# Sliding-window attention feeding a two-matmul network: which engine adds 1e-9 to the softmax sums

## The chip, the cores and the metric

One core of one Trainium2 chip runs the whole program. The metric is the device time of one execution in microseconds (us). A core has five engines that matter here, each with its own queue of instructions worked off in order: TensorE (PE in the rows, PEld for its weight loads), VectorE (DVE), ScalarE (ACT), GpSimd (POOL) and SyncE (SP), which here only issues DMAs. Engines wait for each other through semaphores.

## The reference

Attention over 4 batches, 8 heads, 768 positions, head size 64, with 4 sink keys and a window of 128 keys; then a network with weights 512 by 2048 and 2048 by 512 on the 3072 resulting rows.

```
scores = q @ k.T / sqrt(64);  scores outside sink and window = -1e9
a = exp(scores - max(scores));  a = a / (sum(a) + 1e-9)
x = (a @ v), heads side by side: 3072 x 512
h = x @ w_in;  g = h where h >= 1, 0 where h <= -1, (h+1)^2/4 between
out = g @ w_out
```

All inputs are float32; the weights arrive as 64-bit words and are decoded on the chip.

## The kernel before, in words

The work is cut into 8 chunks of 384 rows (`CT` = 3 tiles of 128 rows). For each chunk the attention of 8 heads is computed, one "unit" for each head, so there are 64 units; then the chunk goes through the network in 16 steps (`NJ`) of 128 hidden columns. Precision is kept by splitting operands in a high part and a rest and multiplying three combinations.

TensorE's queue is written out by hand: `attn_steps` lists the attention pieces of a unit, `moe_steps` those of the network, and `spread` weaves the attention of the next chunk into the network of the present one by fixed costs. The queues of the other engines are ordered by the planner of the framework, which runs its own model of the times when the program is built and puts an instruction where the model has it ready; `queue` and `issue_after` fix that order only in the first part of the program.

Units 0 to 15 take a plain path in pairs (`pair_scores` and the functions after it); there `pair_diag` adds the 1e-9 on VectorE already (L445) and takes the reciprocal behind it (L446). Units 16 to 63 take the "split" path, 48 units:

- `load` fetches q and k by DMA; ScalarE rounds them (L259, L262), VectorE forms the rest of k (L261; GpSimd does so for units 16 to 19), GpSimd the rest of q (L263).
- `scores` runs three times for a unit: two matmuls into a PSUM tile `ps_a` (L277), VectorE's masked maximum (L281, which frees that `ps_a` tile), ScalarE's exponential with the sum as a by-product (L284, an activation and a read of its accumulator). After the third one come the addition of 1e-9 to the three sums of each row (L289, GpSimd), the reciprocal (L290, VectorE), then VectorE's scaling of the probabilities (L296 or L298, the latter an operation with a read of its accumulator) and of the sink part (L301).
- `transp` turns the probabilities around on TensorE (L336, L337) into a `ps_a` tile; ScalarE copies it (L339, L341), VectorE forms the rests (L340, L342), GpSimd cuts two triangles out of each part with selects (L345, L347) and spreads the sinks (L349).
- `values` fetches v; ScalarE rounds it (L313, L318) and GpSimd forms the rests (L314, L319).
- `av` multiplies with v on TensorE (L383); L384 to L386 add the two halves.
- `recheck`, in units 24 to 55, copies one element on GpSimd (L229), re-reads a weight tile by DMA and folds it in on ScalarE and VectorE (L233, L235).

There are three `ps_a` tiles, taken in turn by scores, transposes and values; a matmul into one waits until its last readers are done.

The network of a chunk is `stage1` (L571 on TensorE, L578 and L579 on ScalarE, L580 on VectorE, L581 on ScalarE, L582 on VectorE or GpSimd) and `stage2` (L590 on TensorE). The weights are decoded early by L164 to L177.

Of the kernel before, what the change touches and what calls it, by code (L numbers as in the profile page):

```python
# [13 lines left out]
ALU = mybir.AluOpType  # L14
# [5 lines left out]
CT = 3  # L20
# [29 lines left out]
def attn_ffn(ctx, tc, qk, qkp, vx, vs, par, w_in, w_out, out):  # L50
    nc = tc.nc
# [214 lines left out]
    def scores(u, i):  # L266
        b, h, t0 = u
        qs, k_s = st["qk", u]
        if i == 0:
            st["p", u] = [att.tile([P, CT, 260], F32, name="p"), att.tile([P, 2 * CT], F32, name="stat")]  # L270
        p, stat = st["p", u]
        t = t0 + i
        lo = KB if t == 0 else 0
        c0 = i * KB if t0 else max(0, (i - 1) * KB)
        ps = ps_a.tile([P, 512], F32, name="ps_a")
        for j, q in enumerate(qs):
            nc.tensor.matmul(ps[:, lo:260], lhsT=q[:, i * P:(i + 1) * P], rhs=k_s[:, c0:c0 + 260 - lo],  # L277
                             start=(j == 0), stop=(j == len(qs) - 1))
        peak_i = peak[:, units.index(u), i:i + 1]
        m = (m0, m1, m2)[min(t, 2)]  # L280
        nc.vector.tensor_tensor_reduce(  # L281
            out=p[:, i, lo:260], in0=ps[:, lo:260], in1=m, scale=-0.125, scalar=3.0e38,
            op0=ALU.add, op1=ALU.min, accum_out=peak_i)
        nc.scalar.activation(p[:, i, lo:260], p[:, i, lo:260], AF.Exp, bias=peak_i, scale=-1.0,  # L284
                             accum_out=stat[:, i:i + 1])
        if i < CT - 1:
            return
        st.pop(("qk", u))
        nc.gpsimd.tensor_scalar(stat[:, CT:2 * CT], stat[:, 0:CT], 1.0e-9, None, op0=ALU.add)  # L289
        nc.vector.reciprocal(stat[:, CT:2 * CT], stat[:, CT:2 * CT])  # L290
        i0 = int(t0 == 0)

        for i in range(CT):
            r, own = stat[:, CT + i:CT + i + 1], p[:, i, KB:260]
            if t0 + i == 0:
                nc.vector.tensor_scalar(own, own, r, None, op0=ALU.mult)  # L296
            else:
                nc.vector.tensor_tensor_reduce(out=own, in0=own, in1=p[:, i, 0:P], scale=r, scalar=0.0,  # L298
                                               op0=ALU.add, op1=ALU.add, accum_out=stat[:, i:i + 1])
        sk = att.tile([P, CT * NSINK], F32, name="sk")[:, :(CT - i0) * NSINK]  # L300
        nc.vector.tensor_tensor(sk.rearrange("p (i s) -> p i s", s=NSINK), p[:, i0:, P:KB],  # L301
                                stat[:, CT + i0:2 * CT].unsqueeze(2).broadcast_to([P, CT - i0, NSINK]), op=ALU.mult)
        st["p", u] = (p, sk)
# [244 lines left out]
    def attn_steps(n):  # L548
        us = {k: units[n - k] for k in (-1, 0, 1, 2) if 0 <= n - k < len(units)}
        steps = []  # L550
        if n == NATIVE:
            steps.append((0.0, lambda: load(us[0])))
        if -1 in us:
            steps.append((0.0, lambda: load(us[-1])))
        if 1 in us and n - 1 >= NATIVE:
            steps.append((0.0, lambda: values(us[1])))
        steps += [(0.22, lambda i=i: scores(us[0], i)) for i in range(CT) if 0 in us]
        steps += [(0.43, lambda: transp(us[1]))] if 1 in us and n - 1 >= NATIVE else []
        steps += [(1.0, lambda: av(us[2]))] if 2 in us and n - 2 >= NATIVE else []
        if n in CHECK:  # L560
            steps.append((0.0, lambda: recheck(n - CHECK[0], n)))
        return steps
# [243 lines left out]
```

## Time and profile before

| what | us |
|---|---|
| median of three runs | 717.24 (717.17 to 718.19) |
| the profiled execution, its time | 716.97 |
| the profiled execution, span from first to last instruction | 715.2 |
| TensorE busy | 686.7 |
| VectorE busy | 517.2 |
| ScalarE busy | 496.2 |
| GpSimd busy | 291.5 |

All durations below come from the profiled execution. Its time is 1.8 us more than its span and 0.27 us less than the median of the runs. A row "start, us, engine line operation" gives the start from the beginning of the span and how long it took; a bracket tells how long the engine sat idle before it and what ended the wait. The mean granted TensorE clock is 0.995 of full speed.

### The profile page before, as it was taken

The numbers are of one execution on the slowest core, as the hardware profiler recorded it, in microseconds if no ns is written. First come the engines' busy times: TensorE is split into PE (matmuls) and PEld (weight loads), VectorE is DVE, ScalarE is ACT, GpSimd is POOL, SyncE is SP. The second block draws the span as 40 slices with busy tenths as digits, with TensorE's granted clock in tenths as the row PEclk, the third lists the DMA queues.
The fourth block names the chain that finished last, engine by engine and source line by source line (L and its number), as shares of the span: only waits on it lengthen the run. The fifth ranks groups of instructions, "written<-read, shape, count | busy, mean of one in ns | idle before, by whom it ended". The sixth has DMA issues, their size and how long they took to land.

```text
span 715.2 us, 12306 instructions
## 1 busy us (share of the span) xinstructions
PE 686.7 (96%) x3873; PEld 606.6 (85%) x3873; DVE 517.2 (72%) x1414; ACT 496.2 (69%) x1289; POOL 291.5 (41%) x509
## 2 busy tenths in 40 slices
PE   6689998999999999999999999999999999999996
PEld 3367776799999999999899988999999999989995
DVE  8988997887776878688777787778777777732221
ACT  5786777687677878787677777778776866544332
POOL 2002334754452555366455465646554454400000
PEclk9999999999999999999999999999999999999998
DMA  8854524132243344244433443324422220001001
GB/s 270 278 170 158 177 91 142 52 102 57 58 147 103 117 123 126 65 161 128 110 92 96 141 127 116 111 97 156 120 60 65 80 69 16 8 1 45 1 0 49
DMA packets 44841, 73.04 MB, mean 102 GB/s; under 512 B 13024, under 2 KB 29408, under 8 KB 44768
## 3 DMA queue, kind: packets, MB, share of 16 engines
q1 hardware_dynamic: 41504, 59.59, 27.3%
q10 hardware_dynamic: 3264, 12.58, 5.0%
q8 instruction: 33, 0.54, 0.3%
q14 instruction: 40, 0.33, 0.1%
HBM read 65.87 MB, written 6.29 MB: 101 GB/s over the span
## 4 chain that ended last, share of the span: by engine, by line
PE 76%; DVE 8%; ACT 6%; POOL 3%; DMA 3%; issue 2%; ACTq 0%; SPq 0%; POOLq 0%; DVEq 0%
PE o_ps L590 32%; PE h_ps L571 31%; PE ps_a L383 5%; PE ps_a L277 4%; PE ps_a L336 2%; ACT p L284 1%; POOL q_l L263 1%; DMA r<-qk 1%; PE ps_a L482 1%; DVE bits L173 1%; PE ps_a L463 1%; DVE p L298 1%; PE ps_a L422 1%; ACT p L438 1%; DMA again<-w_out 1%
## 5 line engine op out<-in xcount | busy, mean ns | idle before, releaser
L571 PE MATMUL h_ps<-x,wi 128*128 128x384 f32 x1536 | 309.2, 340 | 0.8 <-DVE g L580 0.8
L571 PEld LDWEIGHTS h_ps<-x,wi 128*128 128x128 f32 x1536 | 262.8, 188 | 10.9 <-issue 1.5
L590 PE MATMUL o_ps<-w,gh 128*128 128x512 f32 x768 | 243.9, 398 | 0.8 <-ACT gh L581 0.8
L590 PE MATMUL o_ps<-w,gl 128*128 128x512 f32 x384 | 150.9, 393 | 0.3 <-POOL gl L582 0.3
L590 PEld LDWEIGHTS o_ps<-w,gh 128*128 128x128 f32 x768 | 134.1, 188 | 18.6 <-issue 2.4
L580 DVE SCALAR_TENSOR_TENSOR g<-g,h_ps 128x384 f32<-128x384 f32 x128 | 70.4, 550 | 64.3 <-ACT g L579 62.8
L578 ACT ACTIVATE g<-h_ps,half 128x384 f32<-128x384 f32 x128 | 73.9, 577 | 55.1 <-PE h_ps L571 54.3
L581 ACT CAST gh<-g 128x384 fp32r<-128x384 f32 x128 | 65.5, 512 | 58.1 <-DVE g L580 57.7
L263 POOL TENSOR_TENSOR q_l<-r,q_h 128x384 fp32r<-128x384 f32 x48 | 48.9, 1018 | 132.8 <-ACT q_h L262 126.8
L582 DVE TENSOR_TENSOR gl<-g,gh 128x384 fp32r<-128x384 f32 x112 | 69.0, 616 | 25.6 <-ACT gh L581 24.8
L590 PEld LDWEIGHTS o_ps<-w,gl 128*128 128x128 f32 x384 | 72.0, 188 | 18.2 <-POOL gl L582 0.8
L284 ACT ACTIVATE p<-p,peak 128x260 f32<-128x260 f32 (+1 forms) x144 | 71.4, 496 | 17.7 <-DVE peak L281 16.8
L261 DVE TENSOR_TENSOR k_s<-k_r,k_s 64x524 fp32r<-64x524 f32 (+1 forms) x44 | 46.4, 1055 | 41.1 <-ACT k_s L259 41.0
L579 ACT ACTIVATE g<-g 128x384 f32<-128x384 f32 x128 | 66.9, 523 | 2.2
L281 DVE CUSTOM_DVE_ANT_0 p<-ps_a,m 128x260 f32<-128x260 f32 (+1 forms) x144 | 56.6, 409 | 15.3 <-PE ps_a L277 14.4
L347 POOL TENSOR_SCALAR_AFFINE_SELECT pt<-pt 128x384 fp32r<-128x384 f32 (+1 forms) x96 | 51.1, 533 | 18.2 <-DVE pt L340 16.2
L298 DVE CUSTOM_DVE_ANT_0 p<-p,stat 128x128 f32<-128x128 f32 x128 | 55.3, 477 | 0.0
L345 POOL TENSOR_SCALAR_AFFINE_SELECT pt<-pt 128x384 fp32r<-128x384 f32 (+1 forms) x96 | 50.4, 525 | 7.1 <-ACT pt L339 3.0
L582 POOL TENSOR_TENSOR gl<-g,gh 128x384 fp32r<-128x384 f32 x16 | 21.3, 1329 | 76.8 <-ACT gh L581 70.8
L383 PEld LDWEIGHTS ps_a<-pt,v_s 128*128 128x128 f32 x304 | 46.6, 188 | 2.2
L383 PE MATMUL ps_a<-pt,v_s 128*128 128x256 f32 (+1 forms) x304 | 47.0, 275 | 0.0
L277 PE MATMUL ps_a<-k_s,q_h 128*128 128x260 f32 (+1 forms) x144 | 40.1, 278 | 1.6 <-DVE sk L342 1.0
(150 smaller groups left out, 983.5 us busy)
## 6 DMA issues: line engine op xcount, KB each, us to landing
r<-qk SPq DMA_DIRECT2D x48, 192.0 KB
k_r<-qk SPq DMA_DIRECT2D x32, 262.0 KB
again<-w_in SPq DMA_DIRECT2D x16, 512.0 KB
again<-w_out SPq DMA_DIRECT2D x16, 512.0 KB
w<-w_in ACTq DMA_DIRECT2D x6, 1024.0 KB
w<-w_out ACTq DMA_DIRECT2D x6, 1024.0 KB
out<-o SPq DMA_DIRECT2D x23, 256.0 KB
r<-vx SPq DMA_DIRECT2D x32, 128.0 KB
```

The source lines that it names most:

```text
L277: nc.tensor.matmul(ps[:, lo:260], lhsT=q[:, i * P:(i + 1) * P], rhs=k_s[:, c0:c0 + 260 - lo], start=(j == 0), stop=(j == len(qs) - 1))
L281: nc.vector.tensor_tensor_reduce(out=p[:, i, lo:260], in0=ps[:, lo:260], in1=m, scale=-0.125, scalar=3.0e38, op0=ALU.add, op1=ALU.min, acc ...
L284: nc.scalar.activation(p[:, i, lo:260], p[:, i, lo:260], AF.Exp, bias=peak_i, scale=-1.0, accum_out=stat[:, i:i + 1])
L298: nc.vector.tensor_tensor_reduce(out=own, in0=own, in1=p[:, i, 0:P], scale=r, scalar=0.0, op0=ALU.add, op1=ALU.add, accum_out=stat[:, i:i ...
L383: nc.tensor.matmul(z, lhsT=w, rhs=y, start=(n == 0), stop=(n == len(mms) - 1))
L571: nc.tensor.matmul(h_ps[:, :T], lhsT=w_i[j][:, w, ct * P:(ct + 1) * P], rhs=x[:, y, ct], start=(ct == 0 and n == 0), stop=(ct == NCT - 1 a ...
L578: nc.scalar.activation(g, h_ps[:, :T], AF.Relu, bias=half, scale=0.5)
L579: nc.scalar.activation(g, g, AF.Square)
L580: nc.vector.scalar_tensor_tensor(g, g, 1.0, h_ps[:, :T], op0=ALU.min, op1=ALU.max)
L581: nc.scalar.copy(gh, g)
L582: (nc.gpsimd if row0 == GL_POOL else nc.vector).tensor_tensor(gl, g, gh.bitcast(F32), op=ALU.subtract)
L590: nc.tensor.matmul(o_ps[tt], lhsT=gg[:, tt * P:(tt + 1) * P], rhs=w_o[j][:, w], start=(j == 0 and n == 0), stop=(j == NJ - 1 and n == 2))
```

## The change

One instruction in `scores`, executed 48 times (once for each unit from 16 to 63), goes from GpSimd's queue to VectorE's. Its operands stay the same: 128 partitions, 3 float32 elements, all in SBUF. The reciprocal is the next line, on VectorE as before.

```
         if i < CT - 1:
             return
         st.pop(("qk", u))
-        nc.gpsimd.tensor_scalar(stat[:, CT:2 * CT], stat[:, 0:CT], 1.0e-9, None, op0=ALU.add)
+        nc.vector.tensor_scalar(stat[:, CT:2 * CT], stat[:, 0:CT], 1.0e-9, None, op0=ALU.add)
         nc.vector.reciprocal(stat[:, CT:2 * CT], stat[:, CT:2 * CT])
```

## Rows read from the trace of the kernel before

**Rows 1.** Busy time of each engine by stretches: the stretch from 124 to 614 us, in which the 48 additions lie, and the sum over three stretches that cover the whole span. Columns: stretch, its length, then busy us (and count) of PE, PEld, DVE, ACT, POOL, granted clock, DMA share and GB/s.
```profile
124.00:614.00 490.00, 485.19 (x2751) 442.34 (x2752) 373.32 (x1097) 366.26 (x956) 255.21 (x453) 1.00 0.33 99
...
sum 715.20, PE 686.74 PEld 606.57 DVE 517.17 ACT 496.22 POOL 291.49; mean PE 228.91 PEld 202.19 DVE 172.39 ACT 165.41 POOL 97.16
```

**Rows 2.** Whom TensorE's matmuls waited for from 100 us to the end: waiting engine and tile, releaser, us in total, times, longest.
```profile
PE ps_a L336 <- DVE p L296: 2.3, 1, 2.3
PE ps_a L336 <- DVE peak L281: 1.2, 3, 0.6
PE ps_a L277 <- DVE sk L342: 1.0, 2, 0.7
PE o_ps L590 <- ACT gh L581: 0.8, 1, 0.8
```

**Rows 3.** The addition by its line (duration in ns: minimum, median, maximum), what its engine waited for (us in total, times), and who waited for it.
```profile
L289 POOL TENSOR_SCALAR stat<-stat x48: 227/230/572, 124.3 to 613.0; 128x3 f32<-128x3 f32 x48
...
  ACT p L284: 14.1, 16
...
  DVE stat L290: 6.6, 14
```

**Rows 4.** The timeline around the first split unit, number 16: its third exponential's accumulator read (L284), its addition's forerunners on GpSimd (L263, L261), VectorE's last work before (L281), the reciprocal, the first scaling and the transpose.
```profile
122.13 1.02 POOL L263 TENSOR_TENSOR q_l<-r,q_h 128x384 fp32r<-128x384 f32 x1 [1.59 <-ACT q_h L262]
...
122.80 0.18 ACT L284 ACTIVATION_READ_ACCUMULATOR p<-p,peak 128x1 f32 x1
...
122.84 0.08 DVE L281 DVE_READ_ACCUMULATOR2_ANT peak<- 128x1 f32 x1
...
123.22 1.01 POOL L261 TENSOR_TENSOR k_s<-k_r,k_s 64x392 fp32r<-64x392 f32 x1
...
124.58 0.18 DVE L290 RECIPROCAL stat<-stat 128x3 f32<-128x3 f32 x1 [1.67 <-POOL stat L289]
...
124.87 0.29 DVE L296 TENSOR_SCALAR p<-p,stat 128x128 f32<-128x128 f32 x1
...
125.22 0.87 PE L336 MATMUL ps_a<-ident,p 128*128 128x128 f32 x3 [2.34 <-DVE p L296]
```

**Rows 5.** The timeline of unit 44: VectorE's rest of k, GpSimd's one-element copy and addition, the reciprocal.
```profile
411.41 1.10 DVE L261 TENSOR_TENSOR k_s<-k_r,k_s 64x524 fp32r<-64x524 f32 x1 [2.50 <-ACT k_s L259]
...
411.88 0.66 POOL L229 COPY again<-peak 1x1 f32<-1x1 f32 x1
...
412.63 0.23 POOL L289 TENSOR_SCALAR stat<-stat 128x3 f32<-128x3 f32 x1
...
412.89 0.18 DVE L290 RECIPROCAL stat<-stat 128x3 f32<-128x3 f32 x1 [0.39 <-POOL stat L289]
```

**Rows 6.** The timeline of unit 35, in the same order, with ScalarE's copy L339 that the first select of the unit before waits for.
```profile
314.54 1.10 DVE L261 TENSOR_TENSOR k_s<-k_r,k_s 64x524 fp32r<-64x524 f32 x1 [0.87 <-ACT k_s L259]
...
314.91 0.47 ACT L339 CAST pt<-ps_a 128x384 fp32r<-128x384 f32 x1
...
315.16 0.57 POOL L289 TENSOR_SCALAR stat<-stat 128x3 f32<-128x3 f32 x1
...
315.76 0.18 DVE L290 RECIPROCAL stat<-stat 128x3 f32<-128x3 f32 x1
```

**Rows 7.** The timeline of unit 45: VectorE's L582 ahead of the reciprocal, and GpSimd's select L345 at the same time.
```profile
421.86 0.56 DVE L582 TENSOR_TENSOR gl<-g,gh 128x384 fp32r<-128x384 f32 x1
422.05 0.74 POOL L345 TENSOR_SCALAR_AFFINE_SELECT pt<-pt 128x384 fp32r<-128x384 f32 x1
...
422.33 0.17 DVE L290 RECIPROCAL stat<-stat 128x3 f32<-128x3 f32 x1
```

**Rows 8.** The same addition where it is on VectorE already, in the pairs of units (L445, 6 elements), with its reciprocal (L446): first a pair with GpSimd idle, then one during a GpSimd instruction (L582).
```profile
17.68 0.17 DVE L445 TENSOR_SCALAR stat<-stat 128x6 f32<-128x6 f32 x1
17.88 0.19 DVE L446 RECIPROCAL stat<-stat 128x6 f32<-128x6 f32 x1
...
65.59 0.71 DVE L445 TENSOR_SCALAR stat<-stat 128x6 f32<-128x6 f32 x1 [0.19 <-ACT pt L438]
...
64.63 1.64 POOL L582 TENSOR_TENSOR gl<-g,gh 128x384 fp32r<-128x384 f32 x1 [4.64 <-ACT gh L581]
```

**Rows 9.** The timeline of unit 22: a GpSimd select that started during VectorE's L582 (179.75 to 180.28), and VectorE's next instruction.
```profile
179.80 0.75 POOL L345 TENSOR_SCALAR_AFFINE_SELECT pt<-pt 128x256 fp32r<-128x256 f32 x1 [0.17 <-ACT pt L339]
180.20 0.43 DVE L296 TENSOR_SCALAR p<-p,stat 128x128 f32<-128x128 f32 x1
```

**Rows 10.** The longest waits of TensorE after 300 us, from the timelines of units 38, 44 and 46.
```profile
350.18 0.36 PE L277 MATMUL ps_a<-k_s,q_h 128*128 128x260 f32 x1 [0.26 <-DVE sk L342]
...
418.47 0.55 PE L336 MATMUL ps_a<-ident,p 128*128 128x128 f32 x3 [0.56 <-DVE peak L281]
...
436.85 0.36 PE L277 MATMUL ps_a<-k_s,q_h 128*128 128x260 f32 x1 [0.74 <-DVE sk L342]
```

**Rows 11.** Two places where TensorE starts just behind VectorE without a recorded wait, from the timelines of units 23 and 45: the freeing of a `ps_a` tile (L342, L281) and the matmul that takes a tile next.
```profile
193.93 0.28 DVE L342 TENSOR_TENSOR sk<-ps_a,sk 8x128 fp32r<-8x128 f32 x1
...
194.35 0.36 PE L277 MATMUL ps_a<-k_s,q_h 128*128 128x260 f32 x1
...
428.17 0.08 DVE L281 DVE_READ_ACCUMULATOR2_ANT peak<- 128x1 f32 x1
...
428.33 0.53 PE L336 MATMUL ps_a<-ident,p 128*128 128x128 f32 x3
```

More of the change, by code (lines that the diff above doesn't have):

```diff
@@ L288, in scores @@
         st.pop(("qk", u))
-        nc.gpsimd.tensor_scalar(stat[:, CT:2 * CT], stat[:, 0:CT], 1.0e-9, None, op0=ALU.add)
+        nc.vector.tensor_scalar(stat[:, CT:2 * CT], stat[:, 0:CT], 1.0e-9, None, op0=ALU.add)
         nc.vector.reciprocal(stat[:, CT:2 * CT], stat[:, CT:2 * CT])
```

## The prediction, made before the changed kernel was built or run

> **What bounds the kernel now.** I first read busy time by stretches. Of the 490 us in which the additions lie, TensorE is busy for 485.19, VectorE for 373, GpSimd for 255 [rows 1]. So TensorE sets the pace, and a change on other engines can win at most the 4.8 us in which it idles there, and can lose only where it makes TensorE wait longer. Next, whom TensorE waits for: 2.3 us once for the first scaled probabilities (L296), 1.2 us in three waits for L281, 1.0 us in two for L342, 0.8 us once for L581 [rows 2]. Nearly all of it hangs on VectorE being late. Last I looked at the addition itself: 48 times 230 ns by the median, GpSimd waits for the exponential in 16 of them, and VectorE's reciprocal waits for the addition in 14, 6.6 us together [rows 3]. In the other 34 VectorE comes later than the addition, or at the same moment. The question is thus which of the 14 waits TensorE feels, and what the 34 lose when VectorE has one more instruction ahead of the reciprocal.
>
> **What is removed and added.** GpSimd loses 48 instructions, VectorE gains 48. No DMA, no matmul and no ScalarE instruction moves. The kind that is added exists already: L445 takes 0.17 us and its reciprocal starts 0.20 us after it started [rows 8], which I take for 3 elements as well. An instruction that need not wait starts some 0.09 us before its predecessor is recorded as ended (the reciprocal at 422.33 against L582's end at 422.42) [rows 7]. So on a free VectorE the reciprocal will start about 0.11 us after the end of the instruction ahead of the pair. The wait for the exponential is not new: the addition waited for it before, and VectorE for the addition. Behind the waiting addition stand the reciprocal, the scalings L296 or L298, L301, L340 and L342, and behind these TensorE's transposes and its next `ps_a` tile.
>
> The price has a second part. The one L445 that met a GpSimd instruction took 0.71 instead of 0.17 us and ended at 66.30, 0.03 us after GpSimd's L582 ended (64.63 + 1.64 = 66.27) [rows 8]. Reciprocals are not held so: at 422.33 one ran inside L345 in 0.17 us [rows 7]. And where a select has been held back by VectorE's two-input work, it goes first afterwards: L345 stood from 179.80, VectorE's next L296 then took 0.43 us and ended 0.08 us after the select [rows 9]. Today the reciprocal starts when GpSimd has just finished; the moved addition has no such shelter. Its cost is therefore between 0.11 us after VectorE is free and the end of a select plus 0.11 us.
>
> **Unit by unit.** The cases that matter:
>
> - Unit 16. The third sum is ready at 122.98, VectorE is free at 122.92, but the addition stood on GpSimd behind L263 and L261, so the reciprocal came at 124.58 and TensorE's transpose at 125.22 after 2.34 us idle [rows 4]. With nothing in the way the reciprocal could start at about 123.24, a gain of 1.34 us. But L263 runs until 123.15, and L261 from 123.22 to 124.23. I expect the addition to slip in between these two (reciprocal at 123.25) and L296, which is of the kind that is held, to end at about 124.31 instead of 125.16: 0.85 us gained. If the addition misses that gap, it ends at 124.31 and the gain is 0.24 us. VectorE then also takes unit 17's addition, 0.2 us, ahead of the weight decoding that the next wait (0.8 us for L581) [rows 2] depends on. I take 0.6 us for what is left, with ends of 0 and 1.34.
> - Units like 44, thirteen of them: 6.6 us in 14 waits, less 1.67, is 0.38 us each. GpSimd's L229 delays the addition; VectorE is free at 412.51 and the reciprocal starts at 412.89 [rows 5]; after the change at about 412.62, 0.27 us earlier. Of these clusters unit 44 ends in a wait of TensorE of 0.56 us [rows 10]; 0.27 us of it should go. The others are covered by slack.
> - Units like 35. L289 lasts 0.57 us because it stands behind VectorE's L261 (314.54 to 315.64), and the reciprocal starts 0.12 us after L261 ends [rows 6]. With the addition on VectorE that is 0.11 us: no change, as in units 38 and 46, where TensorE has waits of 0.26 and 0.74 us [rows 10]. In unit 35, however, ScalarE's L339 ends at 315.38, before L261 does, so GpSimd's next select will be standing there and may go first, some 0.5 us. No wait of TensorE follows that cluster, so I cost it at nothing: slack behind matmuls hides it, and if that is gone it costs up to 0.5 us.
> - Units like 45, in which VectorE comes last. The reciprocal starts 0.09 us before L582 ends; after the change 0.11 us after it, or, with L345 held by L582 and going first, at 422.90 (422.79 + 0.08 + 0.03): 0.2 to 0.57 us late [rows 7]. I take 0.57, since the select stands there as in [rows 9]. TensorE follows VectorE there by 0.08 us (428.25 to 428.33), so it feels all of it; in unit 23 by 0.14 us (194.21 to 194.35) [rows 11], where I take 0.2. Together 0.77 us lost.
>
> **The sum.** -0.6 - 0.27 + 0.77 = -0.1 us. Against the profiled execution's own 716.97 that is 716.9; the runs' median is 0.27 us above the profiled one, so 717.1. About 0.2% (1.4 us) is what a measurement of this kernel can tell from no change; this is far below it. GpSimd should be busy about 16 us less, VectorE 8 to 16 us more than the 517 now [rows 1], neither felt by TensorE.
>
> What no row shows is the order that the planner gives the queues when one instruction changes sides. I bound it by the waits for L281 and L342, 2.2 us, which could all go [rows 2], and by a like amount that could come.
>
> **Rivals.**
>
> 1. *GpSimd goes first everywhere.* The mechanism is that of [rows 8, 9], the place is the end of L261 or L582 in each of the 34 units. It decides where TensorE follows with no slack: units 38, 45 and 46 lose 0.57 us each, unit 23 0.2; in unit 16 the addition misses the gap and the rest is used up by unit 17's; in unit 44 the select behind L229 takes the 0.27 us. That is 1.9 us: 717.24 + 1.9 = 719.1, slower. For it: L445's 0.71 us. Against it: in units like 38 and 46 VectorE's L261 ends before the next select is ready, so there should be nothing to go first. The Trainium skill (SBUF — State Buffer, "SBUF: two separate sides") speaks for it: it calls the pair of ports that VectorE and GpSimd share an exclusive lock, held for the whole instruction by whichever starts first. By that rule the trace's 0.71 us is the normal price of any meeting, and this rival's time would hold.
> 2. *The queues fall better.* Unit 16 gains the whole 1.34 us, and VectorE's cluster comes out so that the waits for L281 and L342 shrink by half or more (1.1 to 2.2 us): 717.24 - 2.4 to - 3.5, so 713.7 to 714.8, faster. For it: these waits are short and depend on VectorE being late by tenths. Against it: only one of them lies behind a unit in which the reciprocal waits for GpSimd.
> 3. *The moved work was never on the path.* TensorE is 99% busy in the stretch, all of the 14 waits but one are 0.38 us, and nothing is felt: 717.2. It differs from my forecast only in unit 16, by tenths.
>
> The Trainium skill (GPSIMD Engine Reference, "Engine selection") sends elementwise work to VectorE rather than GpSimd. By that alone every unit would gain and none lose, -1.34 - 0.27, which is 715.6; the rows of unit 45 speak against its holding here.
>
> **How the numbers follow.** My forecast and rival 3 together, the time staying within 0.2%: 0.62. Rival 1 and other ways of losing more than 1.4 us: 0.21. Rival 2, or an order that gives a part of it with the whole of unit 16: 0.17. The predicted time is 717.1. The range reaches down to 714.9, my forecast less the 2.2 us of waits, and up to 719.6, rival 1 with half a microsecond more for clusters that I cost at nothing.
>
> **What would show it.** Right: L445-like rows on VectorE with a median near 0.16 us and a tail of 0.4 to 0.8 us; no wait of VectorE for GpSimd at the reciprocal; unit 16's transpose at about 124.3; the wait in unit 44 smaller; the cluster of unit 45 later. TensorE's idle time between 124 and 614 us stays near 4.8 us. It would be wrong if that idle time changed by more than 1.4 us, above all if VectorE's or GpSimd's instructions stand in another order than before, if the additions were long throughout (rival 1), or if TensorE's waits for L281 and L342 were gone (rival 2).

## The result, and the profile of the changed kernel

The changed kernel takes 721.75 us by the median of five runs (721.08 to 722.9), the kernel before 718.12 beside it (five runs, 717.17 to 718.75): a ratio of 1.0055, interval 1.004 to 1.007. It is slower by 0.55%; the prediction was 717.1, with a range up to 719.6.

The profiled execution took 722.9 us with a span of 721.2. Busy time of the stretch that holds the additions, and the sum over three stretches that cover the span; columns as in [rows 1].

```profile
124.00:614.00 490.00, 483.80 (x2725) 438.67 (x2724) 384.00 (x1139) 363.21 (x953) 239.77 (x405) 1.00 0.33 100
...
sum 722.00, PE 691.95 PEld 609.26 DVE 530.77 ACT 494.74 POOL 277.12; mean PE 230.65 PEld 203.09 DVE 176.92 ACT 164.91 POOL 92.37
```

GpSimd lost 14.4 us of busy time and VectorE gained 13.6, about as forecast. TensorE's idle time in the stretch went from 4.81 to 6.20 us. Whom TensorE waited for, from 100 us on, in the form of [rows 2]:

```profile
PE ps_a L277 <- DVE sk L342: 2.7, 5, 1.2
PE ps_a L336 <- DVE p L296: 1.5, 1, 1.5
PE ps_a L336 <- DVE peak L281: 1.3, 4, 0.5
PE o_ps L590 <- DVE gl L582: 0.5, 1, 0.5
```

The wait for L296 (unit 16) shrank from 2.3 to 1.5, the one for L581 is gone, and the waits for L342, the last instruction of a unit's work on VectorE, grew from 1.0 in two to 2.7 in five. The moved addition by its line, as in [rows 3]:

```profile
L289 DVE TENSOR_SCALAR stat<-stat x48: 154/374/575, 125.2 to 618.5; 128x3 f32<-128x3 f32 x48
...
  ACT p L284: 1.6, 1
```

Only 18 of the 48 additions took 154 to 174 ns, the price of a free one. The other 30 took 258 to 575. In 29 of these it is GpSimd's select L345 that holds the addition: it had started 0.03 to 0.39 us ahead (in unit 24 the copy L229 was still running, and the select came next), and the addition ends 0.02 to 0.03 us behind it. The longest one, in unit 18, ends so behind L263. In 15 of the 29 the select follows L229 at once, as in unit 44 below; in 14 it had been standing while VectorE ran L261, L580 or L582, as in units 35 and 45.

Five places show how, each to be set beside the group of before. First unit 16 [rows 4]:

```profile
124.29 1.01 POOL L263 TENSOR_TENSOR q_l<-r,q_h 128x384 fp32r<-128x384 f32 x1 [1.59 <-ACT q_h L262]
...
125.17 0.17 DVE L289 TENSOR_SCALAR stat<-stat 128x3 f32<-128x3 f32 x1
125.37 0.18 DVE L290 RECIPROCAL stat<-stat 128x3 f32<-128x3 f32 x1
125.37 1.01 POOL L261 TENSOR_TENSOR k_s<-k_r,k_s 64x392 fp32r<-64x392 f32 x1
...
125.58 0.88 DVE L296 TENSOR_SCALAR p<-p,stat 128x128 f32<-128x128 f32 x1
...
126.52 0.93 PE L336 MATMUL ps_a<-ident,p 128*128 128x128 f32 x3 [1.49 <-DVE p L296]
```

The addition slips in between L263 and L261, L296 is held until L261 is over, and TensorE waits 1.49 us instead of 2.34. Then unit 44 [rows 5]:

```profile
414.10 1.10 DVE L261 TENSOR_TENSOR k_s<-k_r,k_s 64x524 fp32r<-64x524 f32 x1 [1.80 <-ACT k_s L259]
414.56 0.67 POOL L229 COPY again<-peak 1x1 f32<-1x1 f32 x1
415.19 0.51 POOL L345 TENSOR_SCALAR_AFFINE_SELECT pt<-pt 128x384 fp32r<-128x384 f32 x1
415.23 0.51 DVE L289 TENSOR_SCALAR stat<-stat 128x3 f32<-128x3 f32 x1
415.77 0.18 DVE L290 RECIPROCAL stat<-stat 128x3 f32<-128x3 f32 x1
```

The addition no longer stands between L229 and the select on GpSimd, so the select follows L229 at once. It starts 0.04 us ahead of the addition, and the addition ends when the select does (415.74, 415.70). From the end of VectorE's L261 to the reciprocal it was 0.38 us before and is 0.57 now; the forecast was 0.11. Unit 35 [rows 6]:

```profile
317.47 1.09 DVE L261 TENSOR_TENSOR k_s<-k_r,k_s 64x524 fp32r<-64x524 f32 x1 [0.90 <-ACT k_s L259]
317.85 0.46 ACT L339 CAST pt<-ps_a 128x384 fp32r<-128x384 f32 x1
318.38 0.56 POOL L345 TENSOR_SCALAR_AFFINE_SELECT pt<-pt 128x384 fp32r<-128x384 f32 x1 [0.38 <-ACT pt L339]
318.59 0.37 DVE L289 TENSOR_SCALAR stat<-stat 128x3 f32<-128x3 f32 x1
319.00 0.18 DVE L290 RECIPROCAL stat<-stat 128x3 f32<-128x3 f32 x1
```

Here the select stands ready while L261 runs, and the reciprocal comes 0.44 us after L261's end instead of 0.12. Unit 45 [rows 7]:

```profile
424.68 0.56 DVE L582 TENSOR_TENSOR gl<-g,gh 128x384 fp32r<-128x384 f32 x1
424.88 0.74 POOL L345 TENSOR_SCALAR_AFFINE_SELECT pt<-pt 128x384 fp32r<-128x384 f32 x1 [0.79 <-ACT pt L339]
425.16 0.48 DVE L289 TENSOR_SCALAR stat<-stat 128x3 f32<-128x3 f32 x1
425.55 0.54 DVE L340 TENSOR_TENSOR pt<-ps_a,pt 128x384 fp32r<-128x384 f32 x1
426.02 0.16 DVE L290 RECIPROCAL stat<-stat 128x3 f32<-128x3 f32 x1
```

The reciprocal starts 0.78 us after L582's end; before it was 0.09 us ahead of it. Some 0.5 us of this is L340, which the new order of VectorE's queue puts between the two. Last unit 46, where VectorE's L261 ends ahead of the select:

```profile
435.91 0.17 DVE L289 TENSOR_SCALAR stat<-stat 128x3 f32<-128x3 f32 x1
436.02 0.52 POOL L345 TENSOR_SCALAR_AFFINE_SELECT pt<-pt 128x384 fp32r<-128x384 f32 x1 [0.80 <-ACT pt L339]
```

The addition starts 0.11 us ahead of the select and is free; so it is in units 19, 27, 38 and 54, with 0.07 to 0.13 us of lead. The longest of TensorE's waits that answer to [rows 10], in units 38, 44 and 46:

```profile
355.45 0.55 PE L336 MATMUL ps_a<-ident,p 128*128 128x128 f32 x3 [0.30 <-DVE peak L281]
...
421.15 0.55 PE L336 MATMUL ps_a<-ident,p 128*128 128x128 f32 x3 [0.20 <-DVE peak L281]
...
440.70 0.36 PE L277 MATMUL ps_a<-k_s,q_h 128*128 128x260 f32 x1 [1.24 <-DVE sk L342]
```

**Where the time went.** TensorE executes the same matmuls in the same order in both kernels, so the start of one and the same matmul can be compared (us; the number counts the matmuls of a line from 0):

```
matmul                before   after   difference
L571 #24               50.07   52.21   +2.14
L277 #3               118.07  120.22   +2.15
L590 #130 (unit 17)   138.09  139.13   +1.04
L277 #50  (unit 23)   194.35  196.25   +1.90
L277 #75              238.75  241.71   +2.96
L277 #136             341.23  344.19   +2.96
L277 #160             387.82  391.17   +3.35
L277 #180 (unit 44)   425.18  427.86   +2.68
L277 #200             456.73  460.71   +3.98
L277 #230             511.94  515.91   +3.97
L277 #250             541.56  547.07   +5.51
L680 #0               637.76  643.26   +5.50
```

The first 2.14 us arise before any changed instruction runs and differ from execution to execution (last section). From there on the changed kernel loses 3.36 us, about what the medians say (0.55% is 3.95). It gains 1.11 around units 16 and 17, 0.42 at 350 us (unit 38) and 0.67 around unit 44, and loses the rest in steps of 0.1 to 0.8: at 155, 158, 194.35, 235, 237.5, 370, 372, 428, 437, 521, 523.6 and 531 us of the time of before. Little of this is seen as idle time (6.34 us before and 6.62 after, from L571 #24 to L680 #0): 1.5 us are lost while TensorE is busy at a lower clock (see theory 3), and the recorded end of the matmul ahead covers the beginning of a wait, so that the step of 0.65 at 428 us shows as 0.49 idle.

### The profile page after: what moved, and what is told of

Same layout as the page of the kernel before. It is cut to its first block, busy times and chain, and to the rows that moved or that the text cites. A ratio compares the mean times of both kernels' runs of the same rounds, so it can differ in the third digit from the quotient of the medians.

```text
span 721.2 us, 12308 instructions
## 1 busy us (share of the span) xinstructions
PE 692.0 (96%) x3873; PEld 609.3 (84%) x3873; DVE 530.8 (74%) x1462; ACT 494.7 (69%) x1289; POOL 277.1 (38%) x461
## 4 chain that ended last, share of the span: by engine, by line
PE 69%; DVE 15%; ACT 6%; DMA 4%; issue 3%; POOL 1%; SPq 0%; ACTq 0%; POOLq 0%; DVEq 0%
PE h_ps L571 29%; PE o_ps L590 28%; PE ps_a L383 4%; PE ps_a L277 3%; DMA r<-qk 2%; DVE k_s L261 2%; DVE p L298 2%; PE ps_a L336 2%; DVE gl L582 2%; ACT k_s L259 1%; ACT p L284 1%; DVE pt L340 1%; PE ps_a L482 1%; DMA w<-w_in 1%; DVE g L580 1%
## 5 line engine op out<-in xcount | busy, mean ns | idle before, releaser
L571 PE MATMUL h_ps<-x,wi 128*128 128x384 f32 x1536 | 311.9, 342 | 0.6 <-DVE g L580 0.6
L571 PEld LDWEIGHTS h_ps<-x,wi 128*128 128x128 f32 x1536 | 265.3, 190 | 11.3 <-issue 1.5
L590 PE MATMUL o_ps<-w,gh 128*128 128x512 f32 x768 | 244.0, 399 | 0.0
L590 PE MATMUL o_ps<-w,gl 128*128 128x512 f32 x384 | 151.3, 394 | 0.5 <-DVE gl L582 0.5
L590 PEld LDWEIGHTS o_ps<-w,gh 128*128 128x128 f32 x768 | 134.0, 188 | 17.8 <-issue 2.4
L580 DVE SCALAR_TENSOR_TENSOR g<-g,h_ps 128x384 f32<-128x384 f32 x128 | 70.4, 550 | 66.3 <-ACT g L579 64.5
L581 ACT CAST gh<-g 128x384 fp32r<-128x384 f32 x128 | 65.5, 512 | 60.2 <-DVE g L580 59.5
L263 POOL TENSOR_TENSOR q_l<-r,q_h 128x384 fp32r<-128x384 f32 x48 | 48.8, 1018 | 133.1 <-ACT q_h L262 120.0
L582 DVE TENSOR_TENSOR gl<-g,gh 128x384 fp32r<-128x384 f32 x112 | 70.4, 628 | 25.0 <-ACT gh L581 24.1
L590 PEld LDWEIGHTS o_ps<-w,gl 128*128 128x128 f32 x384 | 72.1, 188 | 18.8 <-DVE gl L582 1.4
L284 ACT ACTIVATE p<-p,peak 128x260 f32<-128x260 f32 (+1 forms) x144 | 71.3, 496 | 18.8 <-DVE peak L281 18.0
L261 DVE TENSOR_TENSOR k_s<-k_r,k_s 64x524 fp32r<-64x524 f32 (+1 forms) x44 | 44.9, 1019 | 41.7 <-ACT k_s L259 41.6
L281 DVE CUSTOM_DVE_ANT_0 p<-ps_a,m 128x260 f32<-128x260 f32 (+1 forms) x144 | 56.2, 408 | 11.3 <-PE ps_a L277 10.4
L347 POOL TENSOR_SCALAR_AFFINE_SELECT pt<-pt 128x384 fp32r<-128x384 f32 (+1 forms) x96 | 50.3, 524 | 35.8 <-DVE pt L340 30.3
L298 DVE CUSTOM_DVE_ANT_0 p<-p,stat 128x128 f32<-128x128 f32 x128 | 61.7, 526 | 0.1
L345 POOL TENSOR_SCALAR_AFFINE_SELECT pt<-pt 128x384 fp32r<-128x384 f32 (+1 forms) x96 | 49.5, 516 | 30.4 <-ACT pt L339 30.4
L582 POOL TENSOR_TENSOR gl<-g,gh 128x384 fp32r<-128x384 f32 x16 | 22.5, 1406 | 75.0 <-ACT gh L581 69.0
L277 PE MATMUL ps_a<-k_s,q_h 128*128 128x260 f32 (+1 forms) x144 | 40.4, 281 | 3.2 <-DVE sk L342 2.7
```

Source lines behind the costliest of these rows:

```text
L261: eng.tensor_tensor(k_s[D:P], k_r[D:P], k_s[D:P].bitcast(F32), op=ALU.subtract)
L571: nc.tensor.matmul(h_ps[:, :T], lhsT=w_i[j][:, w, ct * P:(ct + 1) * P], rhs=x[:, y, ct], start=(ct == 0 and n == 0), stop=(ct == NCT - 1 a ...
L580: nc.vector.scalar_tensor_tensor(g, g, 1.0, h_ps[:, :T], op0=ALU.min, op1=ALU.max)
L581: nc.scalar.copy(gh, g)
L582: (nc.gpsimd if row0 == GL_POOL else nc.vector).tensor_tensor(gl, g, gh.bitcast(F32), op=ALU.subtract)
L590: nc.tensor.matmul(o_ps[tt], lhsT=gg[:, tt * P:(tt + 1) * P], rhs=w_o[j][:, w], start=(j == 0 and n == 0), stop=(j == NJ - 1 and n == 2))
```

## Experiments

The first theories: (1) the cost comes from the new order of the queues: not counting the additions, 29 of the 1414 VectorE instructions in the trace stand elsewhere, 14 of 1289 on ScalarE, 7 of 461 on GpSimd and 2 of SP's 301 DMAs; (2) it comes from the addition itself, held on VectorE behind GpSimd's select (the "port theory" of the later expectations, as (1) is their "order theory"); (3) it is the chance of the TensorE clock after unit 16. To part them, the order of every queue was held by edges from each instruction to the next that add no wait, taken from before ("old order") or after ("new order"). Each kernel was timed in five rounds (the repeat of the VectorE kernel in three) against the kernel before; ratios are to that. Its median beside them was 718.07 us for "VectorE, first timing", "GpSimd", "none, old" and "none, free", 718.96 for "VectorE, second timing", "none, new", "second reciprocal" and "twice", and 717.66 for "ScalarE". The ratio is not simply the quotient of the two medians, which is 1.0114 for "twice" and 1.0032 for the second timing.

```diff
-    other_v = nc.values_load(other, min_val=0, max_val=1)
+    hold_order(nc, tc); other_v = nc.values_load(other, min_val=0, max_val=1)
```

The table stands here for all of them; "from L571 #24" is the time in the trace from that matmul to L680 #0 (one execution), "reciprocal" the mean over the 48 units from the end of the third exponential's accumulator read to the reciprocal's start, "waits" TensorE's for L342 and L281 together from 136 us on.

```
addition                     order  median  ratio  interval          from L571 #24  reciprocal  waits
GpSimd (before)              old    718.07  1                        587.69         0.82        2.2
VectorE (after)              new    721.75  1.0055 1.004  to 1.007   591.05         1.00        4.0
VectorE, first timing        old    722.55  1.0057 1.0038 to 1.0076  -
VectorE, second timing       old    721.28  1.0047 1.0026 to 1.0067  589.87         0.98        3.2
GpSimd                       new    718.06  1.0004 0.9983 to 1.0025  586.75         0.90        2.1
none                         old    716.9   0.9976 0.9957 to 0.9995  585.96         0.63        1.1
none                         new    716.01  0.9961 0.9941 to 0.9981  584.97         0.66        1.5
none                         free   719.75  1.0022 1.0002 to 1.0042  589.38         0.58        2.0
second reciprocal instead    new    718.98  1.0003 0.9982 to 1.0025  585.84         0.85        1.7
twice on VectorE             new    727.14  1.0129 1.0104 to 1.0153  597.92         1.25        9.1
ScalarE                      new    717.61  0.9994 0.9975 to 1.0014  587.32         0.68        2.5
```

**The addition on VectorE, before's order.** The edit is the change itself, with each addition right ahead of its reciprocal and all else as before. The second run is the same kernel, for a profile (the first one's profiled execution took 2376 us and is not used).

> The addition is on VectorE as in the changed kernel, but all other instructions stand in the order that they had in the kernel before, on every engine; the addition stands right ahead of its reciprocal. Theory 1, the loss of 3.6 us comes from the order that the planner gave the queues: this one is within 1.5 us of the kernel before, 717 to 719. Theory 2, the loss comes from the instruction itself, held up by GpSimd at the shared SBUF port ahead of the reciprocal: this one is as slow as the changed kernel, 721 to 722.5. Theory 3, chance of when TensorE's clock falls: neither order nor engine decides, and the times of both spread alike over 718 to 722.

> The same kernel as addV_oldorder (the addition on VectorE right ahead of its reciprocal, all else in before's order), for a profile that can be read. Port theory: L289 held with a median over 0.3 us also in this order, reciprocals of units like 35 and 44 later than in the kernel before by 0.1 to 0.4 us, and 721 to 724 us. Order theory: L289 mostly free (0.15 to 0.2 us) and 717 to 719 us.

Measured: 1.0057 and 1.0047, as slow as the change with its own order. The addition by its line:

```profile
L289 DVE TENSOR_SCALAR stat<-stat x48: 159/272/506, 125.1 to 617.6; 128x3 f32<-128x3 f32 x48
```

The median of 0.27 us misses the 0.3 that was named, but 29 of the 48 took over 0.2, each ending 0.02 to 0.03 us behind a select, so it is held in this order too. The order is not needed for the loss.

**The addition on GpSimd, after's order.** The change undone, the order kept:

```diff
-        nc.vector.tensor_scalar(stat[:, CT:2 * CT], stat[:, 0:CT], 1.0e-9, None, op0=ALU.add)
+        nc.gpsimd.tensor_scalar(stat[:, CT:2 * CT], stat[:, 0:CT], 1.0e-9, None, op0=ALU.add)
```

> The addition is on GpSimd as in the kernel before, but all other instructions stand in the order of the changed kernel on every engine. Theory 1 (order): 720.5 to 722.5, as slow as the changed kernel. Theory 2 (the instruction on VectorE): 717 to 719, as the kernel before. Theory 3: anything in 718 to 722.

Measured: 1.0004. Theory 1 falls: the new order by itself costs nothing that shows (at most 0.25%, by the interval). Unit 44 in this kernel, to be set beside that of after above:

```profile
411.82 1.08 DVE L261 TENSOR_TENSOR k_s<-k_r,k_s 64x524 fp32r<-64x524 f32 x1 [2.17 <-ACT k_s L259]
...
413.02 0.23 POOL L289 TENSOR_SCALAR stat<-stat 128x3 f32<-128x3 f32 x1
413.29 0.17 DVE L290 RECIPROCAL stat<-stat 128x3 f32<-128x3 f32 x1 [0.39 <-POOL stat L289]
413.32 0.52 POOL L345 TENSOR_SCALAR_AFFINE_SELECT pt<-pt 128x384 fp32r<-128x384 f32 x1
```

Addition and select stand in one queue, so they never meet, and the reciprocal, which a select does not hold, is 0.39 us after L261's end. The wait that looks like the loss (9.1 us in 18 waits for the addition in this kernel) is the cheaper arrangement.

**No addition.** The addition of 1e-9 is left out; first in before's order, then with the planner free, then in after's order.

```diff
-        nc.gpsimd.tensor_scalar(stat[:, CT:2 * CT], stat[:, 0:CT], 1.0e-9, None, op0=ALU.add)
-        nc.vector.reciprocal(stat[:, CT:2 * CT], stat[:, CT:2 * CT])
+        nc.vector.reciprocal(stat[:, CT:2 * CT], stat[:, 0:CT])
```

> The addition of 1e-9 is left out and the reciprocal reads the sums themselves; all other instructions stand in the order of the kernel before. Theories 1 and 2: 716 to 718, since neither GpSimd's queue nor VectorE holds the reciprocal up; the difference to the addition on VectorE in the old order is the whole price of the added instruction (theory 1: under 1 us; theory 2: 3 us or more).

> The addition of 1e-9 is left out, and the planner orders the queues anew. Theory 1: it differs from the same kernel in the old order by more than 1 us either way, though there is less work than in any other version. Theory 2: it is the same as that one within 1 us, 716 to 718.

> After's order on every engine with the addition of 1e-9 left out. Port theory: without an addition on either engine the order matters little, 716.5 to 718.5 us, as it mattered little with the addition on GpSimd. Order theory in a weaker form (the new order is the worse one as soon as GpSimd has no addition to do): 719.5 to 721.5 us, near the kernel in which the planner was free to order without the addition (719.75).

Measured: 0.9976, 1.0022 and 0.9961. In both held orders the kernel beats the one before, so the addition cost 0.2 to 0.4% on GpSimd already. With the planner free it is slower by 0.2%: an order that the planner chooses can cost as much as the addition. Theory 2 had set this kernel within 1 us of the one in before's order; they are 2.85 apart (719.75 and 716.9), so what theory 1 says of the order in general holds here, though it does not explain the change. In the traces 78 VectorE and 57 GpSimd instructions stand elsewhere than before; the reciprocals come earliest of all (0.58 us), but TensorE waits for other things, from 136 us on:

```profile
PE o_ps L590 <- POOL gl L582: 1.9, 1, 1.9
PE ps_a L277 <- DVE sk L342: 1.8, 3, 1.1
PE ps_a L277 <- DVE xn L386: 1.3, 2, 0.6
```

Which of the moves does it was not tried. TensorE's waits in the fastest of all these kernels, from 136 us on:

```profile
PE ps_a L277 <- DVE sk L342: 1.0, 1, 1.0
PE ps_a L336 <- DVE peak L281: 0.5, 2, 0.3
```

**A second reciprocal in the addition's place.** That left a rival to the holding: that any further instruction of VectorE ahead of the reciprocal costs this much (length theory). Here VectorE has just as many instructions as after the change, in the same order, but none of the kind that is held; the addition of 1e-9 is left out.

```diff
-        nc.vector.tensor_scalar(stat[:, CT:2 * CT], stat[:, 0:CT], 1.0e-9, None, op0=ALU.add)
-        nc.vector.reciprocal(stat[:, CT:2 * CT], stat[:, CT:2 * CT])
+        nc.vector.reciprocal(stat[:, CT:2 * CT], stat[:, 0:CT])
+        nc.vector.reciprocal(stat[:, CT:2 * CT], stat[:, 0:CT])
```

> After's order on every engine, held word for word; in the place of the 48 additions on VectorE stands a second reciprocal of the same sums into the same columns (the addition of 1e-9 is left out; the reciprocal behind it writes the same columns again). VectorE has as many small instructions as in the changed kernel, but of a kind that no record has shown waiting for GpSimd (158 to 179 ns in both kernels). Port theory (the moved addition costs because it is held behind GpSimd's select): L289 at 155 to 180 ns throughout and 717 to 719 us. Length theory (any further instruction of VectorE ahead of the reciprocal costs this much): 721 to 722.5 us, as the changed kernel.

Measured: 1.0003, with an interval that does not touch that of the change. The line of the first reciprocal, and unit 44:

```profile
L289 DVE RECIPROCAL stat<-stat x48: 167/176/179, 126.5 to 614.6; 128x3 f32<-128x3 f32 x48
```

```profile
412.79 1.10 DVE L261 TENSOR_TENSOR k_s<-k_r,k_s 64x524 fp32r<-64x524 f32 x1 [2.10 <-ACT k_s L259]
...
413.88 0.51 POOL L345 TENSOR_SCALAR_AFFINE_SELECT pt<-pt 128x384 fp32r<-128x384 f32 x1
413.92 0.18 DVE L289 RECIPROCAL stat<-stat 128x3 f32<-128x3 f32 x1
414.13 0.18 DVE L290 RECIPROCAL stat<-stat 128x3 f32<-128x3 f32 x1
```

The select starts 0.04 us ahead here too, and it holds neither reciprocal: 0.24 us after L261's end, against 0.57. Nothing differs but the kind of the instruction (and that the second reciprocal reads the sums, not the result ahead of it; that is no matter of time, for it starts 0.21 us after the first one, as the reciprocal behind a free addition starts 0.20 or 0.21 us after that). So the holding is nearly the whole loss: 0.52% by the ratios (1.0055 less 1.0003, 3.7 us), 5.2 us by the two traces (591.05 less 585.84), which both have the stretch of lower clock that theory 3 is about. TensorE's wait in unit 46, 1.24 us after the change, is 0.78 here:

```profile
438.38 0.36 PE L277 MATMUL ps_a<-k_s,q_h 128*128 128x260 f32 x1 [0.78 <-DVE sk L342]
```

What an unheld instruction costs against none is less sure: 0.42% by the ratios (1.0003 less 0.9961), but only 0.87 us in the traces (585.84 less 584.97).

**The addition twice.**

```diff
         nc.vector.tensor_scalar(stat[:, CT:2 * CT], stat[:, 0:CT], 1.0e-9, None, op0=ALU.add)
+        nc.vector.tensor_scalar(stat[:, CT:2 * CT], stat[:, 0:CT], 1.0e-9, None, op0=ALU.add)
```

> The changed kernel in its own order with every addition on VectorE made twice, one behind the other (same operands, same result). Port theory: the first is held as before (median 370 ns), the second mostly runs right behind the select that held the first, so it adds its free 0.15 to 0.17 us in a unit, unless the next select takes the port between them: 722.5 to 724.5 us, and the second's median under 0.2 us. Length theory: as much again as the first brought, 724.5 to 726.5 us. If the first's cost came by the clock alone: no change, 721 to 722.5.

Measured: 1.0129, more than either theory gave. The two additions by their lines, and TensorE's waits from 136 us on (L343 is L342 of the other kernels, one line further down):

```profile
L289 DVE TENSOR_SCALAR stat<-stat x48: 161/374/579, 126.3 to 626.5; 128x3 f32<-128x3 f32 x48
```

```profile
L290 DVE TENSOR_SCALAR stat<-stat x48: 168/170/518, 126.5 to 626.7; 128x3 f32<-128x3 f32 x48
```

```profile
PE ps_a L277 <- DVE sk L343: 5.8, 7, 1.2
PE ps_a L337 <- DVE peak L281: 3.3, 6, 0.9
```

The holding is as the port theory had it: the second addition is mostly free. Its price is not: 0.25 us more in each unit (1.25 less 1.00) costs 0.74% (5.3 us), where the 0.34 us between no addition and the changed kernel cost 0.94%. A tenth of a us of lateness thus costs 0.28% at first and 0.30% then, which the intervals do not part. In the traces it gets dearer, 1.8 and 2.8 us for a tenth (584.97, 591.05 and 597.92), and TensorE's waits go from 1.5 to 4.0 to 9.1 us; that slack is being used up is likely, but shown by one execution of each kernel only.

**The addition on ScalarE, after's order**, right behind the third exponential.

```diff
-        nc.vector.tensor_scalar(stat[:, CT:2 * CT], stat[:, 0:CT], 1.0e-9, None, op0=ALU.add)
+        nc.scalar.activation(stat[:, CT:2 * CT], stat[:, 0:CT], AF.Copy, bias=1.0e-9)
```

> After's order on every engine, but the addition of 1e-9 on ScalarE, right behind the third exponential whose sum it waits for anyway; the reciprocal on VectorE then waits for ScalarE. ScalarE has no part in the holding that L289 shows. If what costs is VectorE's own time (it comes later than the exponential in most units, so an addition of 0.2 us on ScalarE is over before VectorE is free): as without the addition, 715.5 to 717.5 us. If every instruction between exponential and reciprocal costs, on whatever engine, since the chain is on the path: as with the second reciprocal on VectorE or the addition on GpSimd, 718 to 719.5 us. If ScalarE's own queue is on the path as well: over 719.5.

Measured: 0.9994, between the expectations. The reciprocal waits for ScalarE only three times:

```profile
  ACT stat L289: 2.3, 3
```

It starts no later than without the addition (0.68 against 0.66 us on the mean), so it is not the chain ahead of the reciprocal that costs the rest; ScalarE's own queue may. In the traces 1.4 of the 2.35 us between the two kernels (587.32 less 584.97) stand around unit 38, where TensorE waits 0.76 us for L342 at L277 #140 and without the addition not at all. Why stays open.

**Theory 3** falls with these runs. Behind unit 16 TensorE falls to 1.2 GHz for about 3.4 us in the traces of after, of both held kernels without the addition, of the second reciprocal and of the doubled addition, so in the fastest and the slowest. Before, then after, from 124 to 132 us (columns as in [rows 1]; the granted clock, 1.00 and 0.79, is the third number from the end):

```profile
124.00:132.00 8.00, 6.65 (x33) 5.68 (x34) 7.31 (x19) 3.80 (x12) 5.89 (x9) 1.00 0.34 91
```

```profile
124.00:132.00 8.00, 6.48 (x27) 5.40 (x26) 7.84 (x24) 5.32 (x17) 6.12 (x5) 0.79 0.51 181
```

In after it costs 1.5 us: the difference to before goes from -1.07 at L337 #0 (126 us) to +0.46 at L571 #176 (128 us). But the second reciprocal has it too and loses nothing, and the VectorE addition in before's order has none and is slow. TensorE had been idle for 1.5 us at unit 16 ahead of the stretch; it was idle as long in the VectorE addition in before's order, the ScalarE addition and the kernel with the planner free, which have none there. In the two kernels with the addition on GpSimd it was idle for 2.3 us and has no such stretch. What decides is not shown, one execution of each kernel being traced.

## Why the prediction was wrong

- **Unit 16**, -0.6 forecast: right in its course (between L263 and L261, L296 held), and the wait shrank by 0.85 as worked out there; by L337 #0 TensorE had gained 1.07 us. The net 1.11 at L590 #130 is partly luck: 1.5 us went to the stretch at 1.2 GHz and 1.4 came back in waits for L581 and L582, terms that the sum does not have. Those waits shrink as well, by 1.1 us, with the addition on GpSimd in after's order, so that gain is not shown to be the addition's. And the first paragraph's "can lose only where it makes TensorE wait longer" is not so: here it lost while busy, behind a wait that had become shorter.
- **Units 45 and 23**, +0.77 forecast: right. TensorE lost 0.65 and 0.29 in the steps at 428 and 194.35 us, and in unit 45 the select went first, as taken. (With the second reciprocal, which nothing holds, the step at 428 is 0.41 already.)
- **Unit 44**, -0.27 forecast: the reciprocal came 0.19 later in place of 0.27 earlier. TensorE did gain there (0.67), but the kernel with the addition on GpSimd in the same order gains it as well (36.66 us from L277 #160 to #180, against 37.36 before and 36.69 after): it came with the queues' order.
- **The step that failed** is what was costed at nothing: that the other clusters "are covered by slack", and that in units like 35 no wait follows. The known terms come to -1.11 - 0.67 + 0.94 = -0.84 by measurement, the whole to +3.36, so what was costed at nothing came to 4.2 us; the second reciprocal puts the holding at 3.7 us by the ratios and 5.2 in the traces. Two things were wrong in it. First, in units like 44 the working took GpSimd's queue as it was and only crossed out the addition. But the addition was what kept the select away: with it gone, the select follows L229 at once and goes first in 15 units. In 14 more it goes first because it stands ready; I had the row for the price [rows 8], saw this in unit 35 and priced it in unit 45 alone. Second, a cluster with no recorded wait behind it has little slack, and a delay that TensorE does not feel at once is handed on: around units 27, 54 and 55 the additions take 0.17 us, unheld, yet TensorE loses 1.1, 0.75 and 0.55 us there against the second reciprocal in the same order. In unit 46, unheld too, TensorE's wait is 1.24 us in place of 0.74 before and 0.78 with the second reciprocal; a single wait is no full measure, though, for without an addition it is 1.04, TensorE having lost less ahead of it.
- **The signs** that the prediction had named worked in part: the additions' median of 374 ns in place of 160 told against it, the idle time between 124 and 614 us did not (1.39 us more, the limit being 1.4).
- **Rival 1** had the mechanism and was priced too low: 719.1, for six units. Its counter-argument holds (in units 38 and 46 the addition is ahead of the select and not held); unit 46 loses 0.50 all the same, and unit 38 gains 0.42. The Trainium skill (SBUF — State Buffer, "SBUF: two separate sides") has the rule, an exclusive lock that goes to whichever instruction starts first, with VectorE's side restricted to certain instructions (a two-port mode, or two inputs in SBUF). Unit 44's select, 0.04 us ahead, with 0.51 us of holding, and unit 46's addition, 0.11 us ahead and free, agree. That an addition of 3 columns is held and a reciprocal is not is shown here by medians of 374 against 176 ns, beside the same select.
- **The Trainium skill's engine table** (GPSIMD Engine Reference, "Engine selection") sends elementwise work to VectorE, but calls GpSimd slower for two inputs only and roughly at line rate for one, as here. The 715.6 that the prediction worked out from it is not borne out: free, the addition took 154 to 174 ns on VectorE against 230 on GpSimd, but with the holding its median was 374.
- **Rivals 2 and 3** fall: the order brings nothing that can be measured with the addition on GpSimd (1.0004, interval 0.9983 to 1.0025), and the moved work was on the path, since leaving it out gains 0.2 to 0.4%.

## What to carry to other kernels

Before an instruction is moved from GpSimd to VectorE, ask what its place in GpSimd's queue was keeping apart: two instructions of one queue never contend, and once one has moved, what stood behind it starts earlier and may meet it. Count every place where the two now meet, and price each at up to the length of the GpSimd instruction, not at that of the moved one. A wait that the trace puts down to the producer can be the cheapest arrangement; the better answer here was to do without the instruction (the sum holds exp(0) = 1, in which float32 does not see 1e-9), in an order that is held.

## What the runs showed of the hardware that was not expected

- A 128x3 reciprocal on VectorE runs beside a GpSimd select at its free speed (167 to 179 ns in all 48 units, in 28 of them with a select running from before its start to after its end), while a 128x3 addition of one input takes up to 0.51 us at the same place (0.58 behind L263).
- The first 50 us vary from execution to execution; the granted clock falls to 0.5 (1.2 GHz) there one to three times, at times that differ, and L571 #24 started between 50.07 and 54.39 us in the ten traces compared. From there to L277 #3 all ten took 68.00 or 68.01 us. So a trace compared from one matmul behind the disturbed part tells more than a whole time, of which twelve or more of one kernel spread over 4 to 8 us. It is still one execution: the stretch at 1.2 GHz behind unit 16 makes 1.5 us, and where the ratios put an unheld instruction at 0.42% (3 us) the traces have 0.87.
